# Moving a phase's second convolution behind its last product, with VectorE evicting that product, in a fused convolution and feed-forward kernel

## The chip, the cores and the metric

The kernel runs on one core of a Trainium2 chip. The metric is the device time of one launch in microseconds. The core has five engines with queues of their own: TensorE (PE in the profile; PEld is its weight loads), VectorE (DVE), ScalarE (ACT), GpSimd (POOL) and SyncE (SP). TensorE writes its results to PSUM, and VectorE or ScalarE must copy them out before the buffer can be used again; in this text such a copy is called an eviction.

## The reference

The input x has 8 sequences of 3904 tokens with 192 channels. First comes a causal convolution along the sequence: the 192 channels form 8 heads of 24, and each head has 7 taps, softmaxed. Then comes a multiplicative feed-forward network over all 31232 tokens:

```python
w = softmax(weight)                    # 8 heads x 7 taps
xc[b, s, h, g] = sum_k w[h, k] * x_pad[b, s + k, h, g]
h = (xc @ w1) * (xc @ w2) @ w3         # 192 -> 1024, product, 1024 -> 1024
out = h @ w_out                        # 1024 -> 192
```

All inputs and the output are float32; the kernel computes in bfloat16 with sums in float32.

## The kernel before

**Layout.** w3 and w_out don't depend on x, so the prologue multiplies them once into `W_sb` (1024 by 192). The tokens are split into two halves, r = 0 and 1, of 15616 tokens, and each half into 31 rounds of 512 tokens (the last has 256). A round R handles 512 tokens of both halves.

**Per round.** `first_product(R)` computes both 1024-wide products of a round in eight steps. Each step has 6 matmuls into a PSUM tile `pa` and 6 into `pb` (line 376). ScalarE copies `pa` to `asb` (line 383); VectorE multiplies `asb` by `pb` into `abT` (line 385). `second_product(R, r)` multiplies `abT` by `W_sb` with 32 matmuls into a PSUM tile `ops` (line 401); ScalarE copies that to `osb` (line 406), and SP sends `osb` to the output (line 409).

**The convolution.** `conv` works on windows of 32 tokens with 32 by 32 tiles of TensorE (line 273). It fills two PSUM tiles `cps` (windows of even and odd number, e = 0 and 1), and its argument `evict` gives the engines that copy them to `convo` (line 281), in order: the first takes e = 0, the second e = 1. A tile whose channels cross a border of 64 is copied in two pieces. When all 8 heads of a block of windows are done, `store(b)` sends the block to an array `rows` in DRAM (line 312). `transposes(R)` later reads a round back, transposed, as `xT` (line 346); `xT` holds four rounds. All of these DMAs stand in SP's queue in the order in which the program issues them. The inputs of the convolution come by DMAs of GpSimd's queue.

**PSUM.** There is one pool `banks` of four buffers of two banks each, used in turn by `pa`, `pb`, `ops` and `cps`. A matmul group that gets a buffer waits until the copy of that buffer's last tile has ended.

**Phases.** After a prologue (the first three rounds, with the weights' preparation between their steps) the order is written out by hand. A phase p of the last loop runs the first products of two rounds (phase 0 has none), and then four second products (the last phase has six), of the two rounds before: n = 0 to 3. `units` lists what is left of the convolution, and `convolve()` does the next unit. In phases 0 and 1 a unit follows products n = 0, 1 and 2; from phase 2 it follows n = 0 and 2, while units last. Phases 2 to 11 have two units each, and phases 12 to 14 none. At a phase's end stand the transposes of up to two rounds.

Of the kernel before, what the change touches and what calls it, by code (L numbers as in the profile page):

```python
# [16 lines left out]
def kernel(  # L17
# [10 lines left out]
    nc = tc.nc  # L28

    B, S, D = x.shape  # L30
# [6 lines left out]
    NS = 2  # L37
    TS = B * S // NS
    CH = 512
    NR = -(-TS // CH)  # L40
# [27 lines left out]
    def banks(name):  # L68
        return psum.tile([128, NS, CH], FP32, tag="banks", name=name)
# [4 lines left out]
    def slot(shape, dtype, name):  # L74
        return stage.tile(shape, dtype, tag="slot", bufs=5, name=name)
# [5 lines left out]
    def shape_of(b):  # L81
        n = SIZES[b] // 4
        m = n // (1 if b < 3 else 2)
        return n, m, n // m
# [6 lines left out]
    def group(r, e):  # L91
        return slice((2 * r + e) * C, (2 * r + e) * C + C)
# [49 lines left out]
    for r in range(NS):  # L142
        p = group(r, 0).start
# [8 lines left out]
        out=diag, in_=diag, pattern=[[-1, 128 + 8]], compare_op=ALU.is_equal,  # L152
# [13 lines left out]
    for i in range(4):  # L166
        d = diag[i * C:i * C + C, i * C + 2 * i:i * C + 2 * i + C]
        nc.vector.tensor_copy(
            out=cmask[i * C:i * C + C],
            in_=bass.AP(tensor=d.tensor, offset=d.offset, ap=[d.ap[0], [1, 2], [1, C]]))  # L170
# [10 lines left out]
    V, A, P = nc.vector.tensor_copy, nc.scalar.copy, nc.gpsimd.tensor_copy  # L181
# [22 lines left out]
    for i in range(4):  # L204
        ps = slice(i * C, i * C + C)
        nc.vector.tensor_copy(out=every[ps],
                              in_=diag[ps, ps].unsqueeze(1).to_broadcast([C, 4, C]))
    nc.vector.reciprocal(out=total, in_=total)
    nc.vector.scalar_tensor_tensor(
        out=share[:, :, 0:K], in0=taps.unsqueeze(1).to_broadcast([H, H, K]), scalar=total,  # L210
        in1=diag[0:H, 0:H].unsqueeze(2).to_broadcast([H, H, K]), op0=ALU.mult, op1=ALU.mult)
    spread = banks("spread")
    for i in range(4):
# [5 lines left out]
        out=wsb, in_=spread[:, 0, 0:2 * H].rearrange("p (h k) -> p h k", h=H)  # L219
# [5 lines left out]
        out=cprod.rearrange("p h k (s two) -> p h k s two", two=2),  # L225
# [8 lines left out]
    for k in range(2):  # L234
# [5 lines left out]
                          in_=bps[:, 0, 0:C * H].rearrange("p (h s) -> p h s", s=C))  # L240
# [8 lines left out]
    def segments(c0, n):  # L249
        out = []  # L250
        while n:
            m = min(n, Q - c0 % Q)
            out.append((c0 // Q, c0 % Q, m))
            c0, n = c0 + m, n - m
        return out

    def conv(b, h0, nh, evict=(nc.scalar.copy,), es=None):
        n, m, E = shape_of(b)
        es = range(E) if es is None else es
        if b not in convo_of:  # L260
            convo_of[b] = work.tile([128, n, NP, NS, Q], BF16, tag="convo", bufs=2, name="convo")
            heads_left[b] = H * E
        convo = convo_of[b]
        wd = nh * G
        cps = {e: banks("cps") for e in es}
        for q in range(nh):
            cs = slice((h0 + q) * G, (h0 + q + 1) * G)
            for j in range(4):
                xb, s = xb_of[b][j]
                for e in es:  # L270
                    for r in range(NS):
                        o = cps[e][j * C:j * C + C, r, 0:m * wd]
                        nc.tensor.matmul(  # L273
                            o.rearrange("p (w g) -> p w g", g=wd)[:, :, q * G:(q + 1) * G],
                            Aband[group(r, e), h0 + q, :], xb[group(r, e), s:s + m, cs],
                            start=True, stop=True)
        for f, e in zip(evict, es):
            src = cps[e][:, :, 0:m * wd].rearrange("p r (w g) -> p r w g", g=wd)
            o = 0
            for k, c0, c in segments(h0 * G, wd):  # L280
                f(out=convo[:, e::E, k, :, c0:c0 + c]  # L281
                    .rearrange("p w r g -> p r w g"), in_=src[:, :, :, o:o + c])
                o += c
        heads_left[b] -= nh * len(es)
        if not heads_left[b]:
            del xb_of[b]
# [3 lines left out]
    def store(b, first=0):  # L290
        stored[0] = tok(FIRST[b] + SIZES[b]) if b + 1 < NB else TS
        n = SIZES[b] // 4
        convo = convo_of[b]
        for j in range(4):
            w = 0
            while w < n:
                i = FIRST[b] + j * n + w
                if i < first:
                    w += 1
                    continue  # L300
                left = WB - 1 - i % WB
                src = convo[C * j:C * j + ST, w:w + max(1, min(n - w, left))]
                src = src.rearrange("s w k r g -> s w (k r g)")
                j0 = tok(i)
                if left == 0:
                    nc.sync.dma_start(out=rows[j0:j0 + LAST, :], in_=src[0:LAST, 0, :])
                    w += 1
                    continue
                m = min(n - w, left)
                dst = rows[j0:j0 + ST * m, :].rearrange("(w s) c -> s w c", s=ST)  # L310
                for s0, s1 in ((0, 16), (16, ST)):
                    nc.sync.dma_start(out=dst[s0:s1], in_=src[s0:s1])
                w += m
# [28 lines left out]
    def transposes(R, first=0):  # L342
        t0, t1 = max(R * CH, first), min((R + 1) * CH, TS)
        a = t0 % RING
        for k in range(NP):
            nc.sync.dma_start_transpose(
                out=xT[k][:, a:a + t1 - t0], in_=rows[t0:t1, k * 128:(k + 1) * 128])
# [9 lines left out]
    def width(R):  # L357
        return min(CH, TS - R * CH)
# [33 lines left out]
            if between and f0 in between:  # L392
                between[f0]()

    def second_product(R, r):
        ab = abT_of[R]
        ng = width(R) // 128
        ops = banks("ops")
        for g in range(ng):
            for jt in range(JT):  # L400
                nc.tensor.matmul(  # L401
                    ops[:, g // 2, (g % 2) * D:(g % 2) * D + D],
                    ab[:, jt, r, g * 128:(g + 1) * 128], W_sb[:, jt, :],
                    start=(jt == 0), stop=(jt == JT - 1))
        osb = slot([128, ng, D], FP32, "osb")
        nc.scalar.copy(out=osb.rearrange("p (a g) d -> p a (g d)", g=2),  # L406
                       in_=ops[:, 0:ng // 2, 0:2 * D])
        t0 = r * TS + R * CH
        nc.sync.dma_start(
            out=out[t0:t0 + ng * 128, :].rearrange("(g p) d -> p g d", p=128), in_=osb)  # L410
        if r == 1:
            del abT_of[R]

    def last_product(R, r):
        ab = abT_of.pop(R)
        for g, f in zip(range(width(R) // 128), (nc.scalar.copy, nc.vector.tensor_copy) * 2):
            ops = banks("ops")
            for jt in range(JT):
                nc.tensor.matmul(  # L419
                    ops[:, 0, 0:D], ab[:, jt, r, g * 128:(g + 1) * 128], W_sb[:, jt, :],  # L420
                    start=(jt == 0), stop=(jt == JT - 1))
            osb = slot([128, D], FP32, "osb")
            f(out=osb, in_=ops[:, 0, 0:D])  # L423
            t0 = r * TS + R * CH + g * 128
            nc.sync.dma_start(out=out[t0:t0 + 128, :], in_=osb)
# [107 lines left out]
    def heads_of(b):  # L533
        return max(n for n in (2, 4, 8) if n * shape_of(b)[1] * G <= CH)

    units = [(b, h, heads_of(b)) for b in range(4, NB) for h in range(0, H, heads_of(b))]
    loads = [(b, e) for b in range(7, NB) for e in range(len(parts_of(b)))]

    def convolve():
        if units:  # L540
            b, h, n = units.pop(0)
            conv(b, h, n, (V, A))
            if h + n == H:
                store(b)

# [2 lines left out]
    for p, rounds in enumerate(phases):  # L548
        for b, h, n in units[:3]:
            for xb, p0, w in zero_rows.pop(b, []):  # L550
                nc.gpsimd.memset(xb[p0:p0 + PAD, w, :], 0.0)
        for j, R in enumerate(rounds):
            first_product(R)
            if j == 0 and loads:
                nb, part = loads.pop(0)
                P(out=pace, in_=abT_of[R][0:1, JT - 1, 1, 0:2])  # L556
                load_x(nb, (part,))
        last = NR if p == len(phases) - 1 else done + 2
        seconds = [(R, r) for R in range(done, last) for r in range(NS)]
        done = last  # L560
        for n, (R, r) in enumerate(seconds):
            (last_product if (R, r) == (NR - 1, NS - 1) else second_product)(R, r)
            if n in (0, 2) or (n == 1 and p < 2):
                convolve()
        while sent[0] < NR and sent[0] <= LAG + 2 * p + 4 and \
                min((sent[0] + 1) * CH, TS) <= stored[0]:
            transposes(sent[0])
            sent[0] += 1
# [32 lines left out]
```

## Time and profile before

| | |
|---|---|
| median of 3 runs (525.77 to 526.16) | 525.81 us |
| profiled execution, its own time | 525.43 us |
| its span in the profile | 523.7 us |
| TensorE busy, share of the span | 518.1 us, 99% |
| VectorE busy, share | 343.2 us, 66% |
| ScalarE busy, share | 335.3 us, 64% |
| copies `osb` of 128x768 on ScalarE | 60 of 800 ns |
| products `abT` of 128x1024 on VectorE | 240 of 1221 ns |
| copies `asb` of 128x1024 on ScalarE | 244 of 1013 ns |
| granted clock of TensorE | 1.00 |

The profile is taken of one execution. Its span runs from the first to the last instruction that it shows; the execution's own time has 1.7 us more around it. Matmuls are pipelined, so that the duration of one is longer than the distance to the next; distances between starts tell what a matmul costs. A phase with two units has 20.8 us of first products and 11.6 us of second products and convolution.

### The profile page before, as it was taken

To read this page: it belongs to the slowest core of one execution; us is meant where nothing else is said; L and a number is where in the kernel's file an instruction comes from. 1 tells how busy PE (TensorE), PEld (TensorE's weight loads), DVE (VectorE), ACT (ScalarE), POOL (GpSimd) and SP (SyncE) were. 2 spreads that over 40 slices of the span, in tenths; PEclk is the share of its full clock that TensorE was granted. 3 is DMA by queue.
4 is the path that set the end of the run, shared out by engine and by line. 5 is a ranking of instruction groups with operands and counts; after the bars stand their busy time and mean duration, and the time that the engine had idled before them with its cause. 6 is when DMAs were issued, how large, how long until landed. Compare 5 with 4: busy or idle time off the path is not lost.

```text
span 523.7 us, 14832 instructions
## 1 busy us (share of the span) xinstructions
PE 518.1 (99%) x6465; PEld 337.7 (64%) x6466; DVE 343.2 (66%) x326; ACT 335.3 (64%) x385; POOL 67.7 (13%) x127
## 2 busy tenths in 40 slices
PE   8999999999999999999999999999999999999997
PEld 3456765847658476584755847557475584856777
DVE  7786459386592965929669295693957829477380
ACT  6866667476674756747577575765757657476562
POOL 8746002013020100302002020020000000000000
PEclk9999999999999999999999999999999999999999
DMA  9999979847799476994679856794318453140304
GB/s 145 159 199 186 165 172 147 167 108 106 147 147 149 96 103 133 142 180 87 100 158 151 158 83 106 141 159 131 53 63 145 100 138 82 61 106 2 121 3 151
DMA packets 135351, 64.83 MB, mean 124 GB/s; under 512 B 87808, under 2 KB 134262, under 8 KB 135286
## 3 DMA queue, kind: packets, MB, share of 16 engines
q1 hardware_dynamic: 92710, 45.92, 41.7%
q0 software_dynamic: 42560, 17.97, 30.7%
q8 instruction: 50, 0.82, 0.6%
q14 instruction: 15, 0.12, 0.1%
q10 hardware_dynamic: 16, 0.00, 0.0%
HBM read 36.22 MB, written 34.80 MB: 136 GB/s over the span
## 4 chain that ended last, share of the span: by engine, by line
PE 96%; DVE 2%; ACT 1%; issue 0%; DVEq 0%
PE ops L401 31%; PE pa L376 30%; PE pb L376 29%; PE cps L273 3%; PE wps L458 1%; DVE abT L385 1%; PE warm L193 1%; PE w3ps L446 1%; ACT asb L383 1%; PE tps L321 0%; DVE ws L179 0%; PE ops L419 0%; DVE convo L281 0%; ACT convo L281 0%; DVE xT L339 0%
## 5 line engine op out<-in xcount | busy, mean ns | idle before, releaser
L385 DVE TENSOR_TENSOR abT<-asb,pb 128x1024 bf16<-128x1024 bf16 x240 | 293.0, 1221 | 85.2 <-ACT asb L383 68.5
L383 ACT CAST asb<-pa 128x1024 bf16<-128x1024 f32 x244 | 247.1, 1013 | 66.0 <-PE pa L376 65.8
L376 PE MATMUL pb<-xT,wn 64*128 64x512 bf16 (+1 forms) x744 | 198.2, 373 | 0.2 <-DVE abT L385 0.2
L376 PE MATMUL pa<-xT,wn 64*128 64x512 bf16 (+1 forms) x744 | 197.6, 373 | 0.2
L376 PE MATMUL pa<-xT,ws 64*128 64x512 bf16 (+1 forms) x744 | 197.7, 373 | 0.0
L376 PE MATMUL pb<-xT,ws 64*128 64x512 bf16 (+1 forms) x744 | 196.0, 373 | 0.0
L376 PEld LDWEIGHTS <-wn 64*128 64x128 bf16 x1488 | 137.8, 94 | 85.1 <-issue 2.3
L376 PEld LDWEIGHTS <-ws 64*128 64x128 bf16 x1488 | 131.2, 94 | 71.2 <-ACT asb L383 0.5
L401 PE MATMUL ops<-W_sb,abT 128*128 128x192 bf16 x1936 | 166.8, 246 | 0.0
L401 PEld LDWEIGHTS <-abT 128*128 128x128 bf16 x1936 | 157.7, 98 | 9.3 <-issue 9.0
L406 ACT COPY osb<-ops 128x768 f32<-128x768 f32 (+1 forms) x61 | 48.5, 794 | 109.9 <-PE ops L401 109.9
L281 DVE CAST convo<-cps 128x320 bf16<-128x320 f32 (+4 forms) x44 | 31.6, 750 | 76.1 <-PE cps L273 73.0
L117 POOL DMA_DIRECT2D xb<-in_x_dram x74 | 48.4, 661 | 13.4 <-DMA xb<-in_x_dram 5.1
L281 ACT CAST convo<-cps 128x640 bf16<-128x640 f32 (+4 forms) x60 | 34.6, 623 | 2.3 <-PE cps L273 2.0
L556 POOL COPY pace<-abT 1x2 bf16<-1x2 bf16 x9 | 1.6, 176 | 249.8 <-DVE abT L385 249.8
L273 PE MATMUL cps<-xb,Aband 32*32 32x240 bf16 (+2 forms) x1344 | 16.9, 238 | 0.2 <-issue 0.2
L273 PEld LDWEIGHTS <-Aband 32*32 32x32 bf16 x1344 | 9.8, 88 | 8.5 <-issue 7.0
L423 DVE COPY osb<-ops 128x192 f32<-128x192 f32 x1 | 0.4, 358 | 11.7 <-PE ops L419 11.7
L193 PE MATMUL warm<-zeros 128*128 128x512 bf16 (+1 forms) x14 | 5.4, 536 | 1.4 <-DVE zeros L140 1.3
L458 PEld LDWEIGHTS <-w3T 128*128 128x128 bf16 x64 | 5.2, 98 | 1.8 <-issue 1.7
L449 DVE COPY w3T<-w3ps 128x2048 bf16<-128x2048 bf16 x4 | 4.9, 1223 | 1.9 <-PE w3ps L446 1.9
L458 PE MATMUL wps<-wo_b,w3T 128*128 128x192 bf16 x64 | 6.0, 246 | 0.2 <-DVE abT L385 0.2
(59 smaller groups left out, 61.8 us busy)
## 6 DMA issues: line engine op xcount, KB each, us to landing
out_dram<-osb SPq DMA_DIRECT2D x60, 384.0 KB
xb<-in_x_dram POOLq DMA_DIRECT2D x44, 240.0 KB, 7.2
rows<-convo SPq DMA_DIRECT2D x18, 240.0 KB
rows<-convo SPq DMA_DIRECT2D x18, 150.0 KB
w3b<-in_moe_w_dram POOLq DMA_DIRECT2D x8, 256.0 KB, 9.3
xT<-rows SPq DMA_TRANSPOSE x84
rows<-convo SPq DMA_DIRECT2D x11, 120.0 KB
xb<-in_x_dram POOLq DMA_DIRECT2D x4, 228.0 KB, 4.2
```

What stands on the lines that cost most here:

```text
L117: nc.gpsimd.dma_start(out=xb[group(r, e), s:s + w, :], in_=bass.AP(tensor=x.tensor, offset=(r * TS + t - PAD) * D, ap=[[D, C], [E * ST * D ...
L193: nc.tensor.matmul(t[:, j % 2, 0:wd], zeros[:, 0:128], zeros[:, 0:wd], start=True, stop=True)
L273: nc.tensor.matmul(o.rearrange("p (w g) -> p w g", g=wd)[:, :, q * G:(q + 1) * G], Aband[group(r, e), h0 + q, :], xb[group(r, e), s:s + m, ...
L281: f(out=convo[:, e::E, k, :, c0:c0 + c] .rearrange("p w r g -> p r w g"), in_=src[:, :, :, o:o + c])
L376: nc.tensor.matmul(p[:, r, f * N:f * N + N], w_of(i, k, r)[rs, ft * 128:(ft + 1) * 128], xT[k][rs, r0:r0 + N], start=(k == 0), stop=(k == ...
L383: nc.scalar.copy(out=asb[:, :, 0:per * N], in_=pa[:, :, 0:per * N])
L385: nc.vector.tensor_tensor(out=ab[:, f0, :, 0:N], in0=asb[:, :, 0:N], in1=pb[:, :, 0:N], op=ALU.mult)
L401: nc.tensor.matmul(ops[:, g // 2, (g % 2) * D:(g % 2) * D + D], ab[:, jt, r, g * 128:(g + 1) * 128], W_sb[:, jt, :], start=(jt == 0), stop ...
L406: nc.scalar.copy(out=osb.rearrange("p (a g) d -> p a (g d)", g=2), in_=ops[:, 0:ng // 2, 0:2 * D])
L446: nc.tensor.transpose(out=tps[:, q * JT + gt, :], in_=w3b[:, gt * 128:(gt + 1) * 128], identity=ident)
L449: nc.vector.tensor_copy(out=w3T_of[j0].rearrange("p q g c -> p (q g) c"), in_=tps)
L458: nc.tensor.matmul(wps[:, q, 0:D], w3T[:, q, gt, :], wo_b[:, gt, :], start=(gt == 0), stop=(gt == JT - 1))
```

## The change

From phase 2 on, the second unit of a phase moves from behind the third second product (n = 2) to behind the fourth (n = 3), which is the last before the next phase's first product. Where that happens, VectorE evicts the fourth product's tile instead of ScalarE, and the unit's two tiles are evicted by ScalarE (e = 0) and VectorE (e = 1), where it was VectorE and ScalarE. Phases 0 and 1, and those without units, stay as they were. The number of matmuls, copies and DMAs is the same. Where the unit ends a block, its stores now stand behind the fourth output DMA in SP's queue, and not ahead of it.

```diff
-    def second_product(R, r):
+    def second_product(R, r, evict=nc.scalar.copy):
...
-        nc.scalar.copy(out=osb.rearrange("p (a g) d -> p a (g d)", g=2),
-                       in_=ops[:, 0:ng // 2, 0:2 * D])
+        evict(out=osb.rearrange("p (a g) d -> p a (g d)", g=2),
+              in_=ops[:, 0:ng // 2, 0:2 * D])
...
-    def convolve():
+    def convolve(evict=(V, A)):
         if units:
             b, h, n = units.pop(0)
-            conv(b, h, n, (V, A))
+            conv(b, h, n, evict)
...
         for n, (R, r) in enumerate(seconds):
-            (last_product if (R, r) == (NR - 1, NS - 1) else second_product)(R, r)
-            if n in (0, 2) or (n == 1 and p < 2):
-                convolve()
+            if (R, r) == (NR - 1, NS - 1):
+                last_product(R, r)
+            elif n == 3 and p > 1 and units:
+                second_product(R, r, V)
+                convolve((A, V))
+            else:
+                second_product(R, r)
+                if n == 0 or (n < 3 and p < 2):
+                    convolve()
```

`V` is `nc.vector.tensor_copy` and `A` is `nc.scalar.copy`.

## The prediction

> **What bounds the kernel now.** I read four views in this order: the page's busy times and its chain that ended last, the waits of TensorE, and then the timeline of all engines around the end of one phase (the page's slices show a granted clock of 9 tenths or more from end to end).
>
> ```profile
> PE 518.1 (99%) x6465; PEld 337.7 (64%) x6466; DVE 343.2 (66%) x326; ACT 335.3 (64%) x385; POOL 67.7 (13%) x127
> ...
> PE 96%; DVE 2%; ACT 1%; issue 0%; DVEq 0%
> ```
>
> TensorE is busy for 518.1 of 523.7 us, and 96% of the chain is its own. The waits of TensorE name only two behind other engines' copies after the start:
>
> ```profile
> PE pb L376 <- DVE abT L385: 0.2, 1, 0.2
> PE wps L458 <- DVE abT L385: 0.2, 1, 0.2
> ```
>
> So in the phases TensorE never waits. Nothing can be gained there but TensorE's own time, and each new wait is paid in full. The timeline of one phase end (start, duration, engine, operation, count):
>
> ```profile
> 262.55 0.42 PE L273 MATMUL cps<-xb,Aband 32*32 32x240 bf16 x32
> 262.66 0.80 ACT L406 COPY osb<-ops 128x768 f32<-128x768 f32 x1 [1.84 <-PE ops L401]
> ...
> 262.91 2.81 PE L401 MATMUL ops<-W_sb,abT 128*128 128x192 bf16 x32
> 263.13 1.16 DVE L281 CAST convo<-cps 128x960 bf16<-128x960 f32 x1 [4.54 <-PE cps L273]
> 263.35 0.96 ACT L281 CAST convo<-cps 128x960 bf16<-128x960 f32 x1
> ...
> 265.65 0.39 PE L376 MATMUL pa<-xT,wn 64*128 64x512 bf16 x1
> ...
> 265.76 0.80 ACT L406 COPY osb<-ops 128x768 f32<-128x768 f32 x1 [1.44 <-PE ops L401]
> ...
> 266.31 0.38 PE L376 MATMUL pb<-xT,wn 64*128 64x512 bf16 x1
> ...
> 266.52 1.01 ACT L383 CAST asb<-pa 128x1024 bf16<-128x1024 f32 x1
> ...
> 267.56 2.52 DVE L385 TENSOR_TENSOR abT<-asb,pb 128x1024 bf16<-128x1024 bf16 x2 [3.28 <-ACT asb L383]
> ...
> 268.90 0.38 PE L376 MATMUL pb<-xT,wn 64*128 64x512 bf16 x1
> ```
>
> Three things are to be seen. The conv block costs TensorE 0.36 us (262.55 to 262.91), but its copies last 1.16 and 0.96 us; now they hide behind the fourth product's 2.74 us (262.91 to 265.65). The first product then begins 0.18 us behind the fourth product's last matmul. And its third pb starts at 268.90, while the first abT it waits for (it takes over the buffer of the first round's pb) ends at 268.78: with the 0.05 us that a waiting TensorE takes after VectorE's end (abT ended at 42.28, the product behind it began at 42.34), the chain pa, asb, abT, pb has only 0.07 us to spare.
>
> **What is removed.** Matmuls, copies and DMAs keep their number; only places and engines change, in ten phases (p = 2 to 11). A change of operand on TensorE costs about 0.1 us. Four products in a row take 10.67 us up to the next pa (the chain's piece at 480.64), which is 4 x 2.64 (32 matmuls at 82.5 ns) + 0.11; two products up to a conv block take 5.38 (257.17 to 262.55), again 0.10 over 2 x 2.64. Before, a phase end runs product, conv, product, pa: from 257.17 to 265.65, that is 5.384 + 0.356 + 2.746 = 8.486 us. Afterwards three products stand in one run, then conv, then pa: 3 x 2.64 + 0.105 + 0.356 = 8.381. One turnover goes: 0.105 us a phase, 1.05 us over ten. This takes conv to pa to cost what conv to product costs. With 240 columns it isn't in the trace; with 120 it is, in the prologue: the next pa starts 0.143 us behind the last conv matmul's start, a product 0.151 us.
>
> ```profile
> 38.58 0.40 PE L273 MATMUL cps<-xb,Aband 32*32 32x120 bf16 x32
> 38.91 0.39 PE L376 MATMUL pa<-xT,wn 64*128 64x512 bf16 x1
> ```
>
> **What is added: two waits.** Take zero at the start of the fourth product's last matmul. Without waits TensorE has the conv block at 0.176, its last matmul at 0.338, pa0 at 0.532 (0.194 later, as at 262.71 to 262.91), pb0 at 1.191 (0.659 later, as 265.65 to 266.31), and then one group each 0.6475: pb2 at 3.781. In the built program pb0 takes the buffer pair of the fourth product, pa1 that of ScalarE's conv tile, pb1 that of VectorE's.
>
> The first wait is pb0 on VectorE's copy. ScalarE's copy starts 0.283 us behind the last matmul's start (262.375 to 262.658), and I take the same for VectorE; its bounds are the 0.336 of its only copy of this kind and the 0.387 to 0.414 behind conv blocks. Its duration at 768 elements isn't in the trace, but the groups give it:
>
> ```profile
> L281 DVE CAST convo<-cps 128x960 bf16<-128x960 f32 x10 | 11.6, 1158 | 30.9 <-PE cps L273 30.9
> ...
> L423 DVE COPY osb<-ops 128x192 f32<-128x192 f32 x1 | 0.4, 358 | 11.7 <-PE ops L419 11.7
> ```
>
> 358 ns for 192 and 1158 for 960 elements are 158 ns + 1.042 ns an element, so 958 ns for 768 (ScalarE needs 800). 0.283 + 0.958 + 0.053 = 1.294: pb0 is 0.103 us late (up to 0.23 by the bounds).
>
> The second wait is pb2 on the chain through ScalarE, which now has the conv tile in front of asb0. ScalarE on an idle queue behind a 240-column conv block isn't in the trace (it always sat behind its osb copy). From below: 0.325 us behind the last start in the prologue's 120-column blocks; from above 0.640, its starts now, each 0.104 before the copy in front ends; I take VectorE's 0.387, which is behind the same blocks. 0.338 + 0.387 + 0.964 = 1.689; the next begins 0.104 before that end, so asb0 at 1.585 instead of 1.396 (0.042 behind pa0's end). Then 1.012 for asb, 0.032, 1.222 for abT, and 0.053: 3.904, which is 0.123 us behind 3.781. Where the tile is evicted in two pieces (0.443 + 0.697 - 0.112 = 1.028), it is 0.187. The two waits don't add: whoever waited at pb0 waits less at pb2, and 0.103 lies inside. Behind VectorE's copy on its queue stand its conv tile (done by about 2.38, while pb1 needs it at 2.49 or later) and abT0, which has asb0 to wait for anyway.
>
> Five of the ten second places are one piece, four are two. The tenth (p = 11) has 64 matmuls of 72 columns, a block of 0.618 us, which puts pb0 at 1.453 and asb0 by 1.658: no wait. Sum of waits: 5 x 0.123 + 4 x 0.187 = 1.36 us.
>
> **What costs nothing.** ScalarE loses ten copies of 0.80 us and VectorE gets ten of 0.96; neither bounds the span, and only the two waits above reach the path. On SP the fourth product's output DMA now stands ahead of the stores and waits for VectorE; the stores (8 to 11 issues) are released by VectorE's conv copy at about 267.4 instead of 264.35, 3 us later, and six transposes queue behind. In this phase those were issued from 275.9 to 286.4, for a first product at 298.1: 11 us of cover, of which 8 remain. POOL's queue is not passed. VectorE's copy needs an output slot last used five products earlier, long landed.
>
> **Sum.** -1.05 + 1.36 = +0.3 us. The profiled execution took 525.43 us (span 523.7), 0.4 below the median of 525.81; on either basis the change is +0.06%, so 526.1 us for the median. About 0.2% (1.05 us) is what a measurement of this kernel can tell from no change.
>
> **A rule weighed against the rows.** The row: 0.36 us of matmuls against 1.16 us of copies, and the chain above. The Trainium skill, TensorEngine Tiling (Array Packing), Performance Considerations, PSUM Bottleneck, says that packing small matmuls speeds up TensorE but not the evacuation of PSUM, which may become the bottleneck, and that both engines should evacuate. The trace agrees on the proportion. Read as throughput alone it would give the second rival's -0.9 us; by the chain of latencies the sum is +0.3.
>
> **Rivals.** First, slower: ScalarE takes the conv tile late. Each further x of delay goes down the chain asb0, abT0, pb2 nine times: the sum is 0.31 + 9x. From x = 0.08 us (a start 0.47 us behind the last conv matmul) it is slower by over 0.2%; at the 0.640 that all its rows on such blocks show, x = 0.253 and the time is 528.4. For it: ScalarE's prologue starts are 0.065 later than VectorE's 0.260 behind 120 columns, which alone would give 526.7. Against it: the 0.640 is explained by the copy in front. Chance 0.18 beyond 0.2%.
>
> Second, faster: the chain's starts overlap better than I add them, and only VectorE's work counts. From zero: 0.283 + 0.958 + 1.158 + 1.222 + 0.053 = 3.674, below 3.781; with two pieces (0.492 + 0.815) 3.823, late by 0.04. Then -1.05 + 4 x 0.04 = -0.9, 524.9 us; without any wait 524.76. For it: TensorE has no wait in any phase now. Against it: pb0's wait follows from one copy alone, and ScalarE's chain has 0.07 to spare. Chance 0.12, of which 0.07 beyond 0.2%.
>
> Third, the later stores push the transposes past 298: each us over the 8 left is 1 us in up to six store phases. Against it: those 8 us. Chance 0.02, counted as slower. That the edit does nothing is excluded: the built program has ten product copies on VectorE and the conv behind the fourth product.
>
> **How the numbers follow.** The forecast (waits and turnover about cancel) has 0.68; it spans 9 x 0.103 - 1.05 = -0.1 to about +1, where ScalarE starts 0.47 behind. The range takes in half of each rival: 525.2 (towards 524.9) to 527.2 (x of about 0.12). Within 0.2%: 0.68 + 0.05 of the second rival = 0.73; slower 0.18 + 0.02 = 0.20; faster 0.07.
>
> **What would show it.** Right: three products of 7.9 us in a row, pa about 0.36 us behind the conv block's start, osb on VectorE x10 at about 958 ns, and new TensorE waits of about 0.1 us at pb behind DVE osb and 0.02 to 0.1 at pb behind DVE abT, in nine phases. Wrong: no such wait (second rival), waits above 0.25 us a phase or a conv copy on ScalarE that starts 0.45 us or more behind the block (first), or a wait of pa on a DMA (third).

## The result, and the profile after

The changed kernel took 526.91 us (median of 22 runs, 526.42 to 527.56) against 525.93 us of the kernel before (22 runs beside them, 525.54 to 527.07): a ratio of 1.0018, with a 95% interval of 1.0011 to 1.0025 (0.6 to 1.3 us). It is slower by about 1 us, which is clear of the noise. That lies inside the predicted range and just inside the 0.2% that the prediction counted as no change, though the interval reaches beyond it. The forecast of 526.1 us was low by 0.8 us, of which 0.1 us lies in the kernel before (525.93 over the 22 runs, 525.81 over the three of them that the prediction rests on). The profiled execution has a span of 524.8 us, against 523.7.

The page of the changed kernel, its busy times, its chain that ended last and two of its groups:

```profile
PE 519.0 (99%) x6466; PEld 348.1 (66%) x6466; DVE 351.0 (67%) x336; ACT 328.1 (63%) x375; POOL 67.5 (13%) x127
...
PE 95%; ACT 2%; DVE 1%; DMA 1%; issue 0%; POOL 0%; DVEq 0%; POOLq 0%
...
L385 DVE TENSOR_TENSOR abT<-asb,pb 128x1024 bf16<-128x1024 bf16 x240 | 292.5, 1221 | 56.4 <-ACT asb L383 39.3
...
L406 DVE COPY osb<-ops 128x768 f32<-128x768 f32 x10 | 9.6, 958 | 67.9 <-PE ops L401 67.9
```

Ten instructions have gone from ScalarE (385 to 375) to VectorE (326 to 336). The copy that no row of before showed takes 958 ns, the very number that the two other sizes gave. TensorE still carries 95% of the chain. Its waits (time in total, times, longest), as far as the first products go:

```profile
PE pb L376 <- DVE abT L385: 0.2, 1, 0.2
```

Read alone, this view says that no wait was added, since the row is the same as before word for word. But it is another wait: in the kernel before it belongs to the pb at 12.91 us, in the prologue, and here to the pb at 247.67 us, which is shown further down. The waits at the phase ends have no row, and are there all the same. A matmul's record outlasts the distance to the next one, so a delay of a tenth of a microsecond leaves no idle time between two records and shows only in the distance of their starts. The timeline of the same phase end as in the prediction, in the changed kernel (start, duration, engine, operation, count):

```profile
266.03 0.42 PE L273 MATMUL cps<-xb,Aband 32*32 32x240 bf16 x32
266.13 0.96 DVE L406 COPY osb<-ops 128x768 f32<-128x768 f32 x1 [6.71 <-PE ops L401]
...
266.38 0.39 PE L376 MATMUL pa<-xT,wn 64*128 64x512 bf16 x1
...
266.60 0.96 ACT L281 CAST convo<-cps 128x960 bf16<-128x960 f32 x1 [2.31 <-PE cps L273]
...
267.01 1.15 DVE L281 CAST convo<-cps 128x960 bf16<-128x960 f32 x1
267.15 0.37 PE L376 MATMUL pb<-xT,wn 64*128 64x512 bf16 x1
...
267.46 1.02 ACT L383 CAST asb<-pa 128x1024 bf16<-128x1024 f32 x1
...
268.51 3.71 DVE L385 TENSOR_TENSOR abT<-asb,pb 128x1024 bf16<-128x1024 bf16 x3 [0.35 <-ACT asb L383]
...
269.79 0.37 PE L376 MATMUL pb<-xT,wn 64*128 64x512 bf16 x1
```

From pa to pb it is now 0.764 us (266.383 to 267.147) where it was 0.658: pb begins 0.054 us behind the end of VectorE's copy (267.093). And pb2, the third pb (269.785), begins 0.054 us behind the end of the first abT (269.731), where it would come 0.05 us earlier in TensorE's own step.

Summed from the starts in the trace, in us (the first products behind phase p's second unit are those of phase p + 1; a two-piece unit is one whose tiles are copied in two pieces):

| phases 2 to 11 | before | after | difference |
|---|---|---|---|
| second products and convolution, ten phases | 116.389 | 115.325 | -1.064 |
| first products behind a one-piece unit (5) | 20.830 each | 20.990 three times, 20.967 twice | +0.76 |
| first products behind a two-piece unit (4) | 20.830 each | 21.028 | +0.79 |
| first products behind p = 11's unit | 20.826 | 20.825 | 0 |
| one more loss, in phase 6's first products, which begin at 233.5 us | | | +0.35 |
| sum | | | +0.84 |

From the first matmul of phase 2's second products to the end of the span, the kernel before took 399.334 us and the changed one 400.177: +0.843. The other 0.2 us between the two spans lie in the prologue and phase 0, where runs of one and the same kernel differ as much (the stretch begins at 124.60 and 124.38 us in the two profiles of the changed kernel). So the experiments are compared below by this stretch, beside their times. The two profiles of the changed kernel repeat it to 0.001 us; the kernel before and two variants of it that lose nothing in their first products lie within 0.12 us of each other.

The loss in phase 6 is what the prediction didn't have. VectorE's timeline there, first in the kernel before and then in the changed one:

```profile
242.91 6.40 DVE L385 TENSOR_TENSOR abT<-asb,pb 128x1024 bf16<-128x1024 bf16 x5
```

```profile
242.10 3.81 DVE L385 TENSOR_TENSOR abT<-asb,pb 128x1024 bf16<-128x1024 bf16 x3
246.40 3.48 DVE L385 TENSOR_TENSOR abT<-asb,pb 128x1024 bf16<-128x1024 bf16 x3 [0.48 <-POOL pace L556]
```

and TensorE's in the changed kernel:

```profile
247.67 0.37 PE L376 MATMUL pb<-xT,wn 64*128 64x512 bf16 x1 [0.17 <-DVE abT L385]
```

The first product of the phase's second round starts at 246.398, 0.441 us behind the end of its asb (245.957). In the neighbouring phases (2 to 10) that is 0.089. Two steps later a pb comes 0.352 us late. The place is in the middle of the first products, far from the moved convolution.

### The profile page after: what moved, and what is told of

It reads as the page before. It is cut to its first block, busy times and chain, and to the rows that moved or that the text cites. A ratio compares the mean times of both kernels' runs of the same rounds, so it can differ in the third digit from the quotient of the medians.

```text
span 524.8 us, 14836 instructions
## 1 busy us (share of the span) xinstructions
PE 519.0 (99%) x6466; PEld 348.1 (66%) x6466; DVE 351.0 (67%) x336; ACT 328.1 (63%) x375; POOL 67.5 (13%) x127
## 4 chain that ended last, share of the span: by engine, by line
PE 95%; ACT 2%; DVE 1%; DMA 1%; issue 0%; POOL 0%; DVEq 0%; POOLq 0%
PE ops L401 31%; PE pa L376 29%; PE pb L376 29%; PE cps L273 3%; DVE abT L385 1%; ACT asb L383 1%; PE wps L458 1%; DMA wn<-in_moe_w_dram 1%; PE w3ps L446 1%; PE tps L321 0%; POOL xb L117 0%; PE ops L419 0%; ACT ws L179 0%; ACT convo L281 0%; ACT xT L339 0%
## 5 line engine op out<-in xcount | busy, mean ns | idle before, releaser
L376 PE MATMUL pb<-xT,wn 64*128 64x512 bf16 (+1 forms) x744 | 200.8, 372 | 0.2 <-DVE abT L385 0.2
L376 PE MATMUL pb<-xT,ws 64*128 64x512 bf16 (+1 forms) x744 | 194.0, 373 | 0.1
L376 PEld LDWEIGHTS <-ws 64*128 64x128 bf16 x1488 | 129.1, 94 | 69.7 <-issue 4.3
L401 PE MATMUL ops<-W_sb,abT 128*128 128x192 bf16 x1936 | 165.1, 246 | 0.0
L406 ACT COPY osb<-ops 128x768 f32<-128x768 f32 (+1 forms) x51 | 40.4, 792 | 95.1 <-PE ops L401 95.1
L406 DVE COPY osb<-ops 128x768 f32<-128x768 f32 x10 | 9.6, 958 | 67.9 <-PE ops L401 67.9
```

The costliest lines, as they stand in the source:

```text
L376: nc.tensor.matmul(p[:, r, f * N:f * N + N], w_of(i, k, r)[rs, ft * 128:(ft + 1) * 128], xT[k][rs, r0:r0 + N], start=(k == 0), stop=(k == ...
L401: nc.tensor.matmul(ops[:, g // 2, (g % 2) * D:(g % 2) * D + D], ab[:, jt, r, g * 128:(g + 1) * 128], W_sb[:, jt, :], start=(jt == 0), stop ...
L406: evict(out=osb.rearrange("p (a g) d -> p a (g d)", g=2), in_=ops[:, 0:ng // 2, 0:2 * D])
```

## The experiments

All times are medians; "from phase 2" is the stretch named above, and its difference is to the 399.334 us of before. The kernel before took 526.03, 525.96 and 525.99 us beside the three groups of runs.

| kernel | us | ratio (95%) | from phase 2 | difference |
|---|---|---|---|---|
| early_pace | 527.01 | 1.0017 (1.0009 to 1.0026) | 400.178 | +0.84 |
| before_early_pace | 525.83 | 1.0000 (0.9991 to 1.0009) | 399.411 | +0.08 |
| all_scalar | 528.53 | 1.0049 (1.0036 to 1.0061) | 402.079 | +2.75 |
| only_vector | 526.40 | 1.0007 (0.9999 to 1.0016) | 399.683 | +0.35 |
| halves | 527.25 | 1.0025 (1.0015 to 1.0034) | 400.640 | +1.31 |
| cut | 530.60 | 1.0090 (1.0077 to 1.0102) | 403.640 | +4.31 |
| halves_cut | 530.29 | 1.0083 (1.0070 to 1.0097) | 403.652 | +4.32 |
| halves_cut_early | 530.19 | 1.0082 (1.0068 to 1.0095) | 403.644 | +4.31 |
| after_again | 526.85 | 1.0016 (1.0007 to 1.0025) | 400.176 | +0.84 |
| after_shift2 | 526.45 | 1.0012 (1.0003 to 1.0021) | 399.794 | +0.46 |
| before_shift8 | 526.25 | 1.0006 (0.9997 to 1.0015) | 399.649 | +0.32 |
| before_shift4 | 525.96 | 0.9998 (0.9989 to 1.0007) | 399.294 | -0.04 |

### Is it GpSimd's pace copy? (early_pace, before_early_pace)

The profile names GpSimd's small copy `pace` (line 556), which reads a product of VectorE, as what ended the idle time before the late product. Both kernels let it read an earlier product; early_pace is the changed kernel, before_early_pace the kernel before.

```diff
-                P(out=pace, in_=abT_of[R][0:1, JT - 1, 1, 0:2])
+                P(out=pace, in_=abT_of[R][0:1, JT - 2, 1, 0:2])
```

> The changed kernel, with GpSimd's pace copy reading the seventh abT step of the round instead of the eighth, so that it runs some 1.3 us earlier and not at the start of the next round. The trace of the changed kernel has new TensorE waits of 0.14 to 0.20 us in nine phases (1.55 us in all, against 1.06 us saved, net +0.49), and one phase in which VectorE began its first product of the second round 0.35 us late, just as GpSimd's pace copy ran. Theory 1 (the waits give +0.49 us, and the rest of the measured +0.95 are such late starts beside the pace copy): before + 0.5 us, and no first product of a second round more than 0.1 us behind its asb. Theory 2 (the rest has another cause): it stays at before + 0.95 us.

> The kernel before with the same one edit, the pace copy one step earlier: the control. Both theories: within 0.15 us of before, since its trace shows no late start beside the pace copy. If the loads that follow the pace copy cost something by coming 1.3 us earlier, it shows here as a difference that has to be taken off the other run.

The copy moved: in early_pace it stands at 245.26, and VectorE's product starts at 246.914, 0.448 us behind the end of its asb (246.466). The late start is where it was, and the stretch from phase 2 is the same to a thousandth of a microsecond. before_early_pace, the control, has no late product; its +0.08 is one delay in phase 5's second products. The theory that blamed the pace copy fell: a releaser that the profile names is the last event before the start, not always its cause.

### Which of the waits are the change's own? (all_scalar, only_vector)

all_scalar keeps the convolution at its new place, but ScalarE copies the fourth product and the conv tiles keep their old engines:

```diff
-                second_product(R, r, V)
-                convolve((A, V))
+                second_product(R, r)
+                convolve((V, A))
```

> The changed kernel with VectorE's copy undone: the fourth second product is evicted by ScalarE, and the moved unit's tiles by VectorE and ScalarE as before. Theory 1 (what ends last is the chain conv tile, asb0, abT0, pb2 through ScalarE): ScalarE reaches the conv tile only behind its 0.80 us copy, 0.98 us behind the fourth product's last matmul instead of 0.75, so that pb2 waits 0.39 us in one-piece phases and about 0.43 in the others: 3.65 us in all, before + 2.6 us; pb0 doesn't wait. Rival (VectorE's late copy of the fourth product, 0.11 us at pb0, is the cost, and the chain has room): before - 0.5 us or so.

ScalarE's timeline at the phase end:

```profile
267.06 0.80 ACT L406 COPY osb<-ops 128x768 f32<-128x768 f32 x1 [1.84 <-PE ops L401]
267.75 0.96 ACT L281 CAST convo<-cps 128x960 bf16<-128x960 f32 x1
268.60 2.04 ACT L383 CAST asb<-pa 128x1024 bf16<-128x1024 f32 x2
```

ScalarE now has the product copy, a conv tile and asb0 in one row, so that asb0 starts at 268.60, 1.30 us behind pa0 (267.31); in the changed kernel that distance is 1.08. pb0 is on time (0.658 us), and the chain is late at pa1 (by 0.156 or 0.220 us; it begins 0.052 us behind the end of ScalarE's conv tile) and at pb2 (by 0.232): 0.394 us a phase with one piece, 0.459 with two, 3.81 in all against a turnover of 1.07. The chain through ScalarE sets the price, as the prediction had it, and VectorE's copy of the fourth product is what keeps the price down.

only_vector leaves the convolution behind the third product, as before, and lets VectorE copy the fourth:

```diff
-            elif n == 3 and p > 1 and units:
+            elif n == 3 and p > 1 and len(units) + (p == 11):
                 second_product(R, r, V)
-                convolve((A, V))
             else:
                 second_product(R, r)
-                if n == 0 or (n < 3 and p < 2):
+                if n in (0, 2) or (n == 1 and p < 2):
                     convolve()
```

> The kernel before with one part of the change alone: in phases 2 to 11 VectorE evicts the fourth second product, while the second unit stays behind the third, evicted by VectorE and ScalarE. Theory 1: VectorE's copy is done 1.24 us behind the last matmul, and its buffer is asked for by the second pb, about 1.9 us behind: no wait, before within 0.1 us. Rival (VectorE's longer copy costs by itself, 0.1 us a phase): before + 1 us.

At the phase ends nothing is late: 20.83 us of first products everywhere, and second products as before. But the loss in phase 6 is there (20.830 to 21.181), and it is the whole of the +0.35. That loss therefore needs neither the moved convolution nor a wait at a phase end; ten instructions more in VectorE's queue are enough.

### Can the copies be shared out? (halves, cut, halves_cut, halves_cut_early)

halves splits the copy of the fourth product: ScalarE takes the first bank, VectorE the second.

```diff
-        evict(out=osb.rearrange("p (a g) d -> p a (g d)", g=2),
-              in_=ops[:, 0:ng // 2, 0:2 * D])
+        if evict is V:
+            for g, f in ((0, A), (1, V)):
+                f(out=osb[:, 2 * g:2 * g + 2, :].rearrange("p g d -> p (g d)"),
+                  in_=ops[:, g, 0:2 * D])
+        else:
+            evict(out=osb.rearrange("p (a g) d -> p a (g d)", g=2),
+                  in_=ops[:, 0:ng // 2, 0:2 * D])
```

> The changed kernel with the fourth product's copy shared: ScalarE copies its first bank (384 elements), VectorE its second. That copy then ends 0.84 us behind the last matmul instead of 1.24, and pb0 is asked for at 1.19. Theory 1 (the two waits lie inside each other, and the chain through ScalarE ends last): pb0's wait of 0.106 us goes, and pb2 waits 0.15 to 0.20 us instead of 0.05 to 0.09; the time stays that of the changed kernel, before + 0.5 us plus what late starts beside the pace copy add. Rival (the waits add): 9 x 0.106 us less than the changed kernel, before - 0.45 us plus the same.

```profile
266.45 0.42 PE L273 MATMUL cps<-xb,Aband 32*32 32x240 bf16 x32
266.55 0.48 ACT L408 COPY osb<-ops 128x384 f32<-128x384 f32 x1 [1.84 <-PE ops L401]
...
267.06 0.56 DVE L408 COPY osb<-ops 128x384 f32<-128x384 f32 x1 [7.23 <-ACT osb L408]
...
267.68 0.37 PE L376 MATMUL pb<-xT,wn 64*128 64x512 bf16 x1
```

No theory had this: the halves run one after the other, VectorE's 0.034 us behind ScalarE's end (267.065 behind 267.031). Together they take 1.07 us instead of 0.958, pb0 comes 0.215 us late instead of 0.105, and then pb2 has no wait left. All nine phases take 21.053 us. So the edit failed as an improvement, but it shows one thing that the prediction assumed: the two waits don't add. ScalarE's asb0 begins 1.08 us behind pa0 as in the changed kernel, and still the wait at pb2 is gone once pb0 has waited longer.

cut gives VectorE three of the ten windows of ScalarE's conv tile; halves_cut does both, and halves_cut_early also has the pace edit above.

```diff
-        for f, e in zip(evict, es):
+        cut = 7 * m // 10
+        jobs = [(f, e, 0, m) for f, e in zip(evict, es)] if evict != (A, V) else \
+            [(A, 0, 0, cut), (V, 0, cut, m), (V, 1, 0, m)]
+        for f, e, u0, u1 in jobs:
...
-                f(out=convo[:, e::E, k, :, c0:c0 + c]
-                    .rearrange("p w r g -> p r w g"), in_=src[:, :, :, o:o + c])
+                f(out=dst[:, u0:u1, k, :, c0:c0 + c]
+                    .rearrange("p w r g -> p r w g"), in_=src[:, :, u0:u1, o:o + c])
```

> The changed kernel with ScalarE's conv tile cut: ScalarE copies 7 of its 10 windows and VectorE the other 3, ahead of its own tile. ScalarE is then free for asb0 about 1.4 us behind the fourth product's last matmul instead of 1.6. Theory 1: pb2's wait goes, pb0's 0.106 us stays in nine phases: 0.95 us of waits against 1.06 saved, before - 0.1 us plus what late starts beside the pace copy add. Rival (the chain through ScalarE isn't what pb2 waits for): as the changed kernel, before + 0.5 plus the same.

> Both edits: the fourth product's copy shared between ScalarE and VectorE, and ScalarE's conv tile cut to 7 of 10 windows. Theory 1: neither pb0 nor pb2 waits, and the saved turnover of 0.106 us a phase remains: before - 1.05 us, plus what late starts beside the pace copy add. Rival (a third wait takes their place, as VectorE's 3.2 us of copies in front of abT0 end about 2.4 us behind): a wait at pb1 or pb2 of 0.05 us or more in the two-piece phases, before - 0.8 us or above.

> Both edits, and the pace copy one step earlier. Theory 1: before - 1.05 us, with neither waits nor late starts. If the late starts beside the pace copy are not what adds the rest of the changed kernel's +0.95 us, this one lies level with the run without the pace edit.

The timeline of cut, at the end of a one-piece phase:

```profile
268.50 0.72 ACT L285 CAST convo<-cps 128x672 bf16<-128x672 f32 x1 [2.31 <-PE cps L273]
...
269.25 1.52 DVE L285 CAST convo<-cps 128x288 bf16<-128x288 f32 x2 [0.26 <-ACT convo L285]
...
270.82 0.37 PE L380 MATMUL pb<-xT,wn 64*128 64x512 bf16 x1 [0.24 <-DVE convo L285]
```

ScalarE's part is short now (0.72 us), but VectorE's first three windows wait for it, VectorE's own tile waits behind them, and pb1 needs that tile's buffer: 0.24 us at pb1, 0.42 us over its usual distance. In a two-piece phase the waits stand at pa1 and pb2 instead (0.26 and 0.22 us). A phase has about 21.43 us of first products in all three kernels, +0.60; with halves some of the wait moves from pa1 and pb1 to pb0 and the sum stays, so it is the end of VectorE's work in this place that counts. All three expectations of a gain fell.

The profile names ScalarE's copy as the releaser of VectorE's in both edits, and releasers are read from semaphores. So the order is a wait in the program, between two copies of one PSUM tile; that the tile is what couples them is argued, not shown, and whether both engines could read it at once no run here shows.

### A place in the queue (after_again, after_shift2, before_shift8, before_shift4)

In early_pace, only_vector, halves and the changed kernel, the late product is entry number 319 of VectorE's queue in the trace (waits on semaphores counted). It is the first product of phase 6's second round. In phases 2 to 10 this product has one wait more than the others, so that its queue stands still until its asb has ended. In the kernel before, products of that kind are at 272, 311 and 346, and none is late; in cut and halves_cut, whose queue is 20 entries longer, none of that kind is late either. So the theory is that the place in the queue matters, not the work. It is told apart by spare instructions: two, eight or four memsets of VectorE in the prologue, read by nobody.

```diff
+    spare = const.tile([128, 16], FP32)
+    for i in range(2):
+        nc.vector.memset(spare[:, i:i + 1], 0.0)
```

(8 and 4 in the kernels built on the one before; after_again has no edit.)

> The changed kernel once more, beside the others of this call. In its trace, and in those of only_vector, early_pace and halves, one product of VectorE begins 0.44 us behind its asb instead of 0.09 and TensorE loses 0.35 us; each time it is instruction number 319 of VectorE's queue in the trace, the first product of a phase's second round, which has one wait more than the others. At 319, 447 and 575 (128 apart, and queue 14 brings packets of 8192 bytes, 128 instructions of 64 bytes) most traces show a start 0.02 to 0.05 us late. Theory 3: every 128 instructions VectorE's sequencer loses some 0.4 us at such a border, which is hidden in the wait for asb unless the border falls on a product whose extra wait is served only at asb's end; the change shifted a border onto one. Expected: before + 0.85 us (0.49 from the waits at pb, 0.35 from the border), and again 0.35 us lost at number 319.

> The changed kernel with two spare one-column memsets on VectorE in the prologue, where it waits for GpSimd anyway. They shift every later instruction of VectorE by two, so that number 319 is an ordinary product. Theory 3: the 0.35 us goes, before + 0.5 us. Rival (the late start belongs to this place in the program, a DMA or GpSimd, and not to the number): before + 0.85 us, with the late start at number 321.

> The kernel before with eight such memsets. In its trace the first product of a second round with the extra wait is number 311; the shift puts it at 319. Theory 3: VectorE begins it 0.4 us behind its asb, TensorE loses 0.35 us, before + 0.35 us, though the conv and all copies are as before. Rival: before, within 0.1 us.

> The kernel before with four such memsets, the control: number 319 stays an ordinary product. Both theories: before within 0.1 us, and no product more than 0.1 us behind its asb.

VectorE's timeline around the place. after_shift2:

```profile
242.83 6.40 DVE L388 TENSOR_TENSOR abT<-asb,pb 128x1024 bf16<-128x1024 bf16 x5
```

before_shift8:

```profile
242.14 3.81 DVE L388 TENSOR_TENSOR abT<-asb,pb 128x1024 bf16<-128x1024 bf16 x3
246.44 3.48 DVE L388 TENSOR_TENSOR abT<-asb,pb 128x1024 bf16<-128x1024 bf16 x3 [0.48 <-POOL pace L559]
```

Two more instructions take the gap out of the changed kernel: five products stand in one run, and the phase has 21.027 us of first products instead of 21.385. Eight more put it into the kernel before, which then loses 0.35 us in the same phase (21.180 for 20.829), at the very entry 319 (311 + 8). Four more do nothing, and after_again has the gap again. The product is the same in all these kernels, and at the places 311, 315, 321 and 327 it is on time. All four traces came out as the place in the queue says. The times point the same way (526.85 and 526.45; 526.25 and 525.96), but their intervals overlap: the traces decide this, not the medians.

With that the sum closes from both sides: the waits and the turnover without the late product are +0.46 us (after_shift2), the late product alone is +0.35 (only_vector), and both together +0.84. No version that was run is faster than the kernel before.

## Why the prediction was right or wrong

**The turnover: right.** -1.064 us against -1.05. Three products stand in one run of 8.025 us, and pa follows the last conv matmul by 0.193 us where 0.194 was taken from the distance to a product.

**The wait at pb0: right.** VectorE started 0.283 us behind the last matmul, took 958 ns and released pb0 0.054 us later: 0.105 us late against 0.103.

**The wait at pb2: the right chain, a little short.** From pa0 to pb2 TensorE loses 0.188 us in a two-piece phase, against 0.187. In a one-piece phase it loses 0.15 us three times and 0.13 twice, against 0.123. The difference between the three and the two is the one value that the trace of before didn't have. In the three, ScalarE took the conv tile 0.413 us behind the last conv matmul (266.190 to 266.603); in the other six phases it started 0.385 to 0.388 us behind (331.171 to 331.558 at the start of phase 9), like the 0.387 that was taken from VectorE. The 0.026 us go down asb0, abT0 and pb2, three times: 0.08 us. The later start is the first rival's mechanism, at a third of the x = 0.08 us from which it would have decided, and in three phases of nine; why those three have it no run shows. Up to pb2 that makes 1.46 us in place of 1.36. Another 0.09 us comes at the end of the first products, for which the prediction had no term: the last pb to the next second product takes 0.760 us instead of 0.747 in each of the nine phases, of which 0.003 is won back behind pb2. Together the nine phases lose 1.55 us.

**What was left out: the queue's entries.** "Matmuls, copies and DMAs keep their number" was true of the kernel and not of one engine's queue. The ten copies on VectorE move all that stands behind them. By 246 us four of them, each with a wait's entry, had moved one product whose lateness TensorE feels by eight places, from 311 to 319, where VectorE begins late. The prediction had no term for it. It is +0.35 us, nearly twice the error of the waits (0.19), and together they are the distance from the predicted +0.31 to the +0.84 of the traces. That the time stayed within the range in spite of it is owed to the range's width, which was set for other rivals, and not to the working.

**The rivals.** The second (throughput decides, -0.9 us) fell: pb0 and pb2 are late in all nine phases. The Trainium skill's PSUM Bottleneck (TensorEngine Tiling (Array Packing), Performance Considerations), by which the copies out of PSUM may become the bottleneck when small matmuls are packed, holds as far as it goes. The trace agrees that the copies and not the matmuls set the price of the moved block (0.36 us of matmuls, 0.96 and 1.15 us of copies). But it is the latency of two engines in a row that does it, at 63% and 67% busy, and not their throughput. The third (later stores) fell too: the stores are issued at 268.22, 2.37 us behind the last product matmul's start as worked out, and TensorE's waits name no DMA. p = 11 has no wait, as worked out.

**What would show it: one sign was wrong.** New waits at pb behind VectorE's osb and abT were to appear in TensorE's waits, in nine phases. They didn't, though they are there; the starts' distances show them. The one that has a row comes from the late product of phase 6.

## What to carry to other kernels

Where TensorE never waits and a chain of copies has less than 0.1 us to spare, a turnover of 0.1 us saved is easily given back: add up the latencies, engine by engine, from the last matmul to the next use of its buffer, and look for small waits in the distances of the starts, not in a view of idle time. When work moves from one engine to another, the queue behind it moves too; before a difference of some tenths of a microsecond is explained by the change, shift the queue by a few spare instructions in both kernels and see whether it stays. And compare the same stretch of two traces: here it repeats within about 0.1 us, where medians of 22 runs leave 0.4 us on either side.

## What the runs showed of the hardware

**A late start at one place of VectorE's queue.** The product at entry 319 begins 0.44 or 0.45 us behind the end of its asb instead of 0.09, in five kernels and six profiles, whatever the pace copy and the convolution do. Where another product stands at 319, or at 447 and 575, 128 and 256 further, it begins 0.02 to 0.05 us later than its neighbours in most traces, and all_scalar has one at 447 that is 0.26 us late without a loss of TensorE's. No run puts another product with the extra wait on one of these places. That a border of instruction blocks is crossed there is argued from these distances and from the page's rows of the queues that bring instructions (packets, MB):

```profile
q8 instruction: 50, 0.82, 0.6%
q14 instruction: 14, 0.11, 0.1%
```

50 packets of 16 KB are 0.82 MB, and 14 packets of 8 KB are 0.11 MB. The Trainium skill, Runtime: NRT & Kernel Launch, Instruction fetch mechanics, says that each engine's instructions come in blocks of 16 KiB, or 256 instructions, and that crossing a border is mostly hidden. That is 64 bytes an instruction, by which 8 KB would be 128 entries; this is an estimate, and it agrees with the distance of the late places. The 16 KB agree with q8 alone, whose 50 packets would hold TensorE's 12932 instructions to within one packet; the packets of q14 are half as large. Mostly hidden agrees, with one exposed border of 0.35 us in 525 us.

That q14's packets go with VectorE's places the packed traces show, which hold the start of every packet: in all 14 profiles exactly one of this queue starts within 5 us of the start of entry 319, 0.67 to 3.20 us behind it, wherever between 242.7 and 252.5 us that entry falls. How the crossing delays the product no run shows.

**A wait of up to 0.23 us that no view of idle time shows**, as told above: 1.55 us in nine phases, and not a row for them. In all_scalar, pb2 is late by 0.232 us in all nine phases, without a row either.
